# Four interleaved attention and linear-attention layers on one core: value products streamed twice, first products repeated, the last key tile alone, priorities moved

## The chip, the core and the metric

The kernel runs on one core of a Trainium2 chip. A core has TensorE (PE in the rows, its weight loads PEld), VectorE (DVE), ScalarE (ACT), GpSimd (POOL) and SyncE (SP, which here only issues DMAs). Each engine works through its own program in order and waits on semaphores for the others. TensorE's clock is granted at one of two levels, 2.4 GHz (1.00 in the rows) or 1.2 GHz (0.50). The metric is the device time of one execution in microseconds.

## What is computed

Activations are 2048 tokens by 512 features in bf16, 32 heads of 16. Two kinds of layer alternate twice, each with a layer norm ahead of it, an output projection and a residual sum behind it:

```python
def A(x):                      # 4 segments of 512 tokens
    q, k, v = x @ wq, x @ wk, x @ wv        # by head
    for s in range(4):
        p = softmax(q_s @ k_s.T * scale + causal mask)
        a_mem = (phi(q_s) @ M) / (phi(q_s) @ z + 1e-6)
        o_s = g * a_mem + (1 - g) * (p @ v_s)
        M, z = M + phi(k_s).T @ v_s, z + sum(phi(k_s))
    return o @ wo
def B(x):                      # all 2048 tokens at once
    q, k, v = split(x @ wqkv)
    f = lambda t: concat(softmax(t @ w_phi), softmax(-t @ w_phi))
    kv, z = f(k).T @ v, sum(f(k))           # over all tokens
    return (f(q) @ kv) / (f(q) @ z + 1e-6) @ wo
x = x + A(norm(x)); x = x + B(norm(x))
x = x + A(norm(x)); x = x + B(norm(x))
```

B needs `kv` and `z` of all 2048 tokens before its first query can be finished, so each pair of layers (L = 0 and L = 1 in the code) has one point where everything waits for the last key tile.

## The kernel before

A token tile is 128 tokens; there are 16, four to a segment. The program is not written in the order in which it runs. `build` records operations in a graph (`Graph.op`), each with engines it may run on, a duration in ns, the tiles that it reads and writes, and a label. `Graph.schedule` plays the graph through a planner: `backward` gives each operation a priority, `forward` lets each engine take the ready operation of best priority whose tiles can be had, and the best of 12 rounds for each of six rules fixes the order of every engine's program. So a changed duration, or a changed priority, moves instructions anywhere.

Products go through `mm`: a list of pairs, one product on the array's lower and one on its upper 64 rows, which run together. In `a_att` the scores of query tile `i` against key tile `j` (label S) are one pair of 512 columns, `D<-pQ,pK` in the rows; ScalarE makes the exponential of 1024 columns of it (`act`, L577), GpSimd masks the diagonal tile (L1005), and the value products (label PV, `D<-pV,p`) have the probabilities as weights and 16 value columns and a column of ones as the moving side: 17 columns for each head, key tile and half, 5120 products in all. VectorE then takes the reciprocal of the sums (L623) and scales (L1033). A PSUM tile `D` has two halves of 512 columns; of a half a PV product group uses the first 136 columns, and where there is a memory term 136 more.

`b_keys` makes the keys and values of B: projections `D<-WB_k,pX` and `D<-WB_v,pX` of two token tiles at a time, exponentials of both signs (label kexp), their sums by head (Zred, L1107), reciprocals (rZ, L623), the scaled values (Vt, L1118), and the products `D<-pT,p` that are summed into `KV32` (L1081). `TOK` says which pairs of tiles of a segment go together: in segments 0 to 2 all four tiles, in segment 3 the first pair, then the second. `b_query` makes the query exponentials (`D<-pX,WB_q`), the denominators (`D<-Rz,p`), the numerators (`D<-Rkv,p`) of each tile, scales them (L1194, L1201) and hands them to `out_proj`, whose products are `D<-WB_o,p` (for A `D<-WA_o,p`). The residual of B is added on VectorE (L1066) for even tiles; for the odd ones (`RES_PE`) TensorE adds it as a fifth product with the identity (`D<-X,ident`), and a copy by ScalarE or VectorE takes the sum back to `X`.

While it plays, `forward` keeps count of the columns that TensorE has streamed lately. Where they are few and the operation is a score pair, the pair is issued twice (`o.again`); the second issue computes the same again. In this program that happens to 24 pairs.

Of the kernel before, what the change touches and what calls it, by code (L numbers as in the profile page):

```python
# [9 lines left out]
ALU = mybir.AluOpType  # L10
# [82 lines left out]

WINDOW, KEEP = 3000.0, 0.45


class Graph:
# [39 lines left out]
    def op(self, ch, reads=(), writes=(), opens=(), kind="c", lat=None, label="", ndma=0, port=False, kb=0, hard=()):  # L137
        o = Op()
        o.id = len(self.ops)
        o.ch = ch  # L140
        o.deps = set()
        o.succ = []
        o.tiles = []
        o.opens = list(opens)
        o.kind = kind
        o.lat = lat
        o.label = label
        o.ndma = ndma
        o.need = False
        o.port = port  # L150
        o.kb = kb
        o.hard = tuple(hard)
        o.cyc = o.again = 0
        o.deps.update(hard)
# [73 lines left out]
    def forward(self, prio, pools, rule):  # L228
# [72 lines left out]
        while len(order) < n:  # L301
# [25 lines left out]
            for e in ENGS:  # L327
# [39 lines left out]
                if e == "pe":  # L367
                    while seen_pe and seen_pe[0][0] < now - WINDOW:
# [37 lines left out]
    def schedule(self, pools, rounds, off):  # L406
# [3 lines left out]
        for rule in RULES:  # L410
# [10 lines left out]
            self.log.append(min(log))  # L421
        self.model_us = self.forward(best[1], pools, best[2]) / 1000.0


    def emit(self):
# [108 lines left out]
class Kernel:  # L534
# [20 lines left out]
    def mm(self, phases, cols, reads, writes, opens=(), label="", after=None):  # L555
# [5 lines left out]
        for n, cs in enumerate(cols):  # L561
            dur = sum(max(c / 2.4 + 2.5, 25.5) for c in cs)

            def fn(e, n=n):
                ins = None
                for pair in phases()[n] * (1 + cell[n].again):
                    for out_ap, lhsT, rhs, st, sp in pair:
                        ins = e.matmul(out_ap, lhsT, rhs, start=st, stop=sp, tile_position=(basep(lhsT), 0))  # L568
                return ins
            last = self.g.op({"pe": (dur, fn)}, reads, writes, opens if n == 0 else (), label=label, hard=(last,) if last else ())  # L570
            last.cyc = sum(cs)
            cell.append(last)
        return last
# [51 lines left out]
    @staticmethod  # L625
    def dur_recip(n):
        return 65 + 6.3 * n

# [190 lines left out]
    def ln(self, t, xT, flex=False, pe=False, root="pool"):  # L819
        R, v = self.R, self.v  # L820
        tt = t % 4
        v(lambda e: e.bn_stats(self.stats[:, t, :], self.X[:, t, :]), 602, [R("X", t)], [R("st", t)], label="bn")  # L822
        v(lambda e: e.bn_aggr(self.mv[:, t, :], self.stats[:, t, :]), 75, [R("st", t)], [R("mv", t)], label="bn")  # L823
        rs = self.rstd[:, t:t + 1]
# [10 lines left out]
        if flex:  # L835
# [3 lines left out]
            self.g.op({"dve": (323, lambda e: e.tensor_scalar(xn.t[:], self.X[:, t, :], self.mv[:, t, 0:1], rs, op0=ALU.subtract, op1=ALU.mult)),  # L839
                       "act": (590, lambda e: e.activation(xn.t[:], self.X[:, t, :], ACT.Identity, scale=rs, bias=nb))},  # L840
                      [R("X", t), R("mv", t), R("rstd", t), R("nb", t)], [xn], label="xn", port=True)
# [23 lines left out]

    def vproj(self, ps, W, wres, tts, xT, opens=(), label=""):
        self.proj(ps, lambda b, h, k: (xT.t[64 * h:64 * h + 64, k, tts[b] * 128:tts[b] * 128 + 128], W[64 * h:64 * h + 64, k, :]), 512,
                  [xT[tt] for tt in tts] + wres, opens, label)
# [107 lines left out]
    def a_att(self, L, s, i):  # L976
# [9 lines left out]
        for hp in range(2):  # L986
# [22 lines left out]
            def phases(PV=PV, PTs=PTs, hp=hp, pvv=pvv):  # L1009
# [17 lines left out]
            self.mm(phases, [[17] * (8 * (i + 1)) + ([68, 4, 68, 4] if nm else []), [17] * (8 * (i + 1))],  # L1027
                    list(PTs.values()) + [PTs[(gg, i)][hh] for gg in range(2) for hh in range(2)] + [VT[j] for j in range(i + 1)]
# [62 lines left out]
    def b_keys(self, L, c, parts):  # L1091
# [4 lines left out]
        for part in parts:  # L1096
            Es, Vts = {}, {}
            for tp in part:
                tts = (2 * tp, 2 * tp + 1)
                S = self.T(self.pD, "gen")  # L1100
                E = Es[tp] = [self.T(self.p2, "ET") for _ in range(2)]
                Z = self.T(self.pS, "Z")
                self.vproj(S, self.WB["k"], [R("WB", "k", i) for i in range(4)], tts, xT, opens=E + [Z], label="BK")
                for sgn in range(2):
                    self.act(lambda sgn=sgn, E=E: E[sgn].t[:], lambda S=S: S.t[:], ACT.Exp, 1024, [S], [E[sgn]],
                             scale=1.0 - 2.0 * sgn, label="kexp")
                    fn = lambda e, sgn=sgn, E=E, Z=Z: e.tensor_reduce(Z.t[:, sgn * 64:(sgn + 1) * 64],  # L1107
                                                                      E[sgn].t[:].rearrange("p (h d) -> p h d", d=16), AX.X, ALU.add)
                    v(fn, 1131, [E[sgn]], [Z[sgn]], label="Zred")
                for b, tt in enumerate(tts):  # L1110
                    Vt = Vts[tt] = self.T(self.pT, "Vt")
                    v(lambda e, Vt=Vt, Z=Z, b=b: self.recip(e, Vt.t[:, :, :, 16, :], Z.t[:, 0:128].rearrange("p (s t g h) -> p s t g h", s=2, t=2, g=NG)[:, :, b]),
                      self.dur_recip(64), [Z[0], Z[1]], [Vt["z"]], label="rZ")
                ps = self.T(self.pD, "gen")
                self.vproj(ps, self.WB["v"], wv + [Vts[tt]["z"] for tt in tts], tts, xT, label="BV")
                for b, tt in enumerate(tts):
                    Vt = Vts[tt]
                    v(lambda e, Vt=Vt, ps=ps, b=b: e.tensor_tensor(  # L1118
                        Vt.t[:, :, :, 0:16, :],
                        ps.t[:, None, b * 512:b * 512 + 512].to_broadcast([128, 2, 512]).rearrange("p s (g d h) -> p s g d h", g=NG, h=8),  # L1120
                        Vt.t[:, :, :, 16:17, :].to_broadcast([128, 2, NG, 16, 8]), ALU.mult), 1131,
                      [ps, Vt["z"]], [Vt["v"]], label="Vt")
            tts = [2 * tp + b for tp in part for b in range(2)]
            for q in range(2):
# [3 lines left out]
                def phases(ps=ps, n=n, s0=s0, tts=tts, Es=Es, Vts=Vts):  # L1128
                    def item(b, h, k, tt, ph):
                        sl = s0 + b * n + k  # L1130
                        return (ps.t[:, 512 * b + k * 136:512 * b + k * 136 + 136],
                                Es[tt // 2][sl % 2].t[64 * h:64 * h + 64, (tt % 2) * 512 + (sl // 2) * 128:(tt % 2) * 512 + (sl // 2 + 1) * 128],
                                Vts[tt].t[64 * h:64 * h + 64, sl % 2, sl // 2, :, :].rearrange("p c h -> p (c h)"),
                                ph == 0 and k == 0 and tt == tts[0], ph == 1 and k == n - 1 and tt == tts[-1])
                    return [[(item(p, 0, k, tt, p), item(1 - p, 1, k, tt, p)) for k in range(n) for tt in tts] for p in range(2)]
                self.mm(phases, [[136] * (n * len(tts))] * 2, [E for tp in part for E in Es[tp]] + [Vts[tt][r] for tt in tts for r in "zv"], [ps], label="KV")
                self.kv_add(ps, q, c == 0 and part[0] == 0, c == 3 and part[-1] == 1)

# [118 lines left out]


def basep(ap):
    st = ap.ap[0][0]  # L1260
# [13 lines left out]
ROUNDS = 12  # L1274
OFF = {"warm": 1e6}
N_WARM = 14
# [38 lines left out]
```

## Time and profile before

| | us |
|---|---|
| median of three runs | 574.87 |
| lowest, highest | 570.24, 577.41 |
| the profiled execution | 577.28 |
| its span, first to last instruction | 575.5 |

The profiled execution stands at the upper end of the runs, 0.4% over their median. Its granted clock, taken over the span, is 0.938 of full speed. A busy share is an average over stages that differ: the start (loads and folding of weights) to some 100 us, attention of the first pair of layers to 240, the point where B waits for its last keys at 260, attention of the second pair to 510 with B's queries of the first in it, the second such point at 534, and B's queries and outputs to the end.

### The profile page before, as it was taken

What the parts mean: (1) busy time and instruction counts of PE and PEld (TensorE: products, weight loads), DVE (VectorE), ACT (ScalarE), POOL (GpSimd) and SP (SyncE); (2) the same over time, 40 slices, a digit from 0 to 9 for tenths busy, and PEclk for the clock granted to TensorE, in tenths of its full rate; (3) what the DMA queues carried; (4) which work ended last, traced back from release to release, by engine and by line L of the source; (5) the groups of instructions that cost most, each with busy time, mean ns of one, the idle gap of its engine ahead of it and who ended that gap; (6) DMA issues with size and microseconds to landing.
All of it is one profiled execution on the core that took longest, in us unless ns stands there. A gap on an engine that the chain in (4) does not pass through costs nothing.

```text
span 575.5 us, 24135 instructions
## 1 busy us (share of the span) xinstructions
PE 487.9 (85%) x10888; PEld 278.5 (48%) x10888; DVE 443.8 (77%) x858; ACT 462.2 (80%) x534; POOL 230.6 (40%) x401
## 2 busy tenths in 40 slices
PE   8788878889899888988798899887988997899776
PEld 3234344444455454446545455453544564345564
DVE  5979878996885957687898877796876885377794
ACT  4969878897999988757799798897987898856663
POOL 5757656426635643001255435651743373110000
PEclk9978889998999999997799898898998999699699
DMA  7294335334111111000124335322121013000245
GB/s 213 50 237 56 85 46 91 52 57 51 27 31 31 31 42 19 2 2 3 44 65 89 75 66 68 66 49 56 40 40 34 17 25 45 1 11 2 40 110 131
DMA packets 90517, 31.72 MB, mean 55 GB/s; under 512 B 77584, under 2 KB 90416, under 8 KB 90416
## 3 DMA queue, kind: packets, MB, share of 16 engines
q1 hardware_dynamic: 90352, 30.17, 26.8%
q8 instruction: 85, 1.39, 1.1%
q14 instruction: 16, 0.13, 0.1%
q0 software_dynamic: 64, 0.02, 0.0%
HBM read 6.32 MB, written 2.10 MB: 15 GB/s over the span
## 4 chain that ended last, share of the span: by engine, by line
PE 48%; DVE 20%; ACT 18%; DMA 9%; issue 4%; POOL 1%; SPq 0%; ACTq 0%; DVEq 0%
PE D L568 46%; ACT p L577 16%; DMA p<-p 7%; DMA pX<-p 2%; DVE p L586 2%; DVE X L1066 2%; DVE stats L822 2%; DVE p L1033 2%; PE D L887 2%; DVE pV L586 1%; DVE p L1194 1%; DVE pQ L939 1%; DVE p L843 1%; DVE pS L623 1%; DVE pS L1107 1%
## 5 line engine op out<-in xcount | busy, mean ns | idle before, releaser
L577 ACT ACTIVATE p<-D 128x1024 bf16<-128x1024 f32 x416 | 400.0, 1036 | 78.3 <-PE D L568 75.2
L1005 POOL TENSOR_SCALAR_AFFINE_SELECT p<-p 128x512 bf16<-128x512 bf16 x256 | 162.1, 659 | 165.9 <-ACT p L577 165.3
L568 PE MATMUL D<-pQ,pK 64*128 64x512 bf16 x688 | 131.3, 399 | 19.3 <-ACT p L577 14.2
L568 PE MATMUL D<-pV,p 64*128 64x17 bf16 x5312 | 92.7, 170 | 4.8 <-issue 3.3
L568 PEld LDWEIGHTS D<-pV,p 64*128 64x128 bf16 x5312 | 82.9, 93 | 18.3 <-issue 6.5
L568 PEld LDWEIGHTS D<-pQ,pK 64*128 64x128 bf16 x688 | 33.4, 96 | 58.8 <-ACT p L577 35.0
L830 POOL TENSOR_SCALAR rstd<-mv 128x1 f32<-128x1 f32 x60 | 17.6, 295 | 100.5 <-DVE mv L823 98.5
L1107 DVE TENSOR_REDUCE pS<-p 128x64 f32<-128x1024 bf16 x32 | 38.3, 1210 | 19.4 <-ACT p L577 19.3
L1066 DVE TENSOR_TENSOR X<-X,D 128x512 bf16<-128x512 bf16 x48 | 32.8, 683 | 26.5 <-PE D L568 26.0
L568 PE MATMUL D<-WA_o,p 64*128 64x256 bf16 x512 | 40.6, 278 | 12.6 <-DMA p<-p 6.8
L568 PE MATMUL D<-WB_o,p 64*128 64x256 bf16 x512 | 41.5, 288 | 9.6 <-DMA p<-p 7.6
L1033 DVE TENSOR_TENSOR p<-D,pS 128x256 bf16<-128x256 f32 x112 | 46.5, 419 | 2.5
L822 DVE BATCH_NORM_STATS2 stats<-X 128x6 f32<-128x512 bf16 x64 | 43.4, 683 | 5.8 <-DMA X<-in_A_x_dram 3.1
L1118 DVE TENSOR_TENSOR pT<-D,pT 128x1024 bf16<-128x1024 f32 x32 | 38.6, 1214 | 6.3 <-PE D L568 6.0
L568 PE MATMUL D<-WB_k,pX 64*128 64x512 bf16 x256 | 34.6, 389 | 6.8 <-issue 4.2
L568 PE MATMUL D<-WA_v,pX 64*128 64x512 bf16 x256 | 36.8, 412 | 3.6 <-DMA pX<-p 1.4
L623 DVE RECIPROCAL pS<-D 128x32 f32<-128x32 f32 (+1 forms) x64 | 20.8, 326 | 21.8 <-PE D L568 21.1
L832 POOL TENSOR_TENSOR rstd<-rstd,mhalf 128x1 f32<-128x1 f32 x60 | 35.6, 595 | 3.8
L568 PEld LDWEIGHTS D<-WA_o,p 64*128 64x128 bf16 x512 | 22.6, 96 | 29.3 <-DMA p<-p 11.3
L568 PE MATMUL D<-WB_v,pX 64*128 64x512 bf16 x256 | 32.8, 378 | 1.5 <-issue 0.7
L568 PE MATMUL D<-pX,WA_q 64*128 64x512 bf16 x224 | 32.6, 416 | 1.5 <-DVE p L1033 0.6
L568 PE MATMUL D<-pX,WB_q 64*128 64x512 bf16 x256 | 33.6, 392 | 0.2
(110 smaller groups left out, 647.6 us busy)
## 6 DMA issues: line engine op xcount, KB each, us to landing
pQ<-p SPq DMA_DIRECT2D x112, 32.0 KB, 1.8
out_dram<-X SPq DMA_DIRECT2D x16, 128.0 KB, 1.9
X<-in_A_x_dram SPq DMA_DIRECT2D x3, 512.0 KB, 6.0
pX<-in_B_wqkv_dram SPq DMA_DIRECT2D x3, 512.0 KB, 5.5
p<-p SPq DMA_TRANSPOSE x76, 2.8
pX<-p SPq DMA_TRANSPOSE x54, 2.7
X<-in_A_x_dram SPq DMA_DIRECT2D x4, 128.0 KB, 2.2
pX<-in_A_wk_dram SPq DMA_DIRECT2D x2, 256.0 KB, 3.7
```

Of the source, the lines that this page charges most:

```text
L568: ins = e.matmul(out_ap, lhsT, rhs, start=st, stop=sp, tile_position=(basep(lhsT), 0))
L577: return self.g.op({"act": (dur, lambda e: e.activation(out_ap(), in_ap(), func, scale=scale))}, reads, writes, opens, label=label)
L586: "dve": ((340 if fast else n / 0.96 + 65), lambda e: e.tensor_copy(out_ap(), in_ap()))}
L623: return e.reciprocal(o, i)
L822: v(lambda e: e.bn_stats(self.stats[:, t, :], self.X[:, t, :]), 602, [R("X", t)], [R("st", t)], label="bn")
L830: v(lambda e: e.tensor_scalar(rs, self.mv[:, t, 1:2], LN_EPS, None, op0=ALU.add), 170, [R("mv", t)], [R("rstd", t)], eng="pool", label="rstd")
L832: v(lambda e: e.tensor_tensor(rs, rs, self.mhalf[:], ALU.pow), 540, [R("rstd", t), R("mhalf")], [R("rstd", t)], eng="pool", label="rstd")
L1005: v(lambda e, pt4=pt4: e.affine_select(pt4(), pt4(), [[0, 4], [1, 128]], ALU.is_ge, 0.0, base=0, channel_multiplier=-1), 560, [PT], [PT[hh ...
L1033: v(lambda e, pvv=pvv, rden=rden, part=part, dst=dst, k=k: e.tensor_tensor(part(dst), pvv()[:, :, k, :, 0:16], rden()[:, :, k, :, None].to ...
L1066: self.v(lambda e: e.tensor_tensor(xt(), xt(), res(), ALU.add), 602, [R("X", t), ps], [R("X", t)], label="res")
L1107: fn = lambda e, sgn=sgn, E=E, Z=Z: e.tensor_reduce(Z.t[:, sgn * 64:(sgn + 1) * 64], E[sgn].t[:].rearrange("p (h d) -> p h d", d=16), AX.X ...
L1118: v(lambda e, Vt=Vt, ps=ps, b=b: e.tensor_tensor(Vt.t[:, :, :, 0:16, :], ps.t[:, None, b * 512:b * 512 + 512].to_broadcast([128, 2, 512]). ...
```

## The change

- A value product streams its 17 columns twice. `twice` gives the moving side a second pass (step 0) and the output a second place 272 columns further on, in columns of the same half that nothing else uses and nobody reads. The products stay 5120, of 34 columns each.
- The planner may repeat any operation whose first pair has 64 columns or more, not only scores: its first pair is issued up to `again` times ahead of the real products, which begin with a start flag and so overwrite it. At most 1024 columns are added to one operation; the planner's own mark (`KEEP`) rises from 0.45 to 0.6, and the value products count with 34 columns.
- In segment 3 `b_keys` works with tiles 12 and 13 as a pair and 14 alone, then 15 alone.
- `RES_PE` holds for all tiles of B, even ones too.
- A few durations of the planner are set anew, and the best priorities are moved by 108 recorded random steps (`STEPS`), so the order is another one throughout.

```diff
-WINDOW, KEEP = 3000.0, 0.45
+WINDOW, KEEP, MORE = 3000.0, 0.6, 2
...
-                    o.again = int(o.label == "S" and now > WINDOW and streamed < KEEP * WINDOW * 2.4)
-                    dur *= 1 + o.again
-                    cyc = o.cyc * (1 + o.again)
+                    o.again = 0
+                    if o.unit >= 64:
+                        lack = KEEP * WINDOW * 2.4 - streamed - o.cyc
+                        o.again = min(MORE * 512 // o.unit, max(0, int(-(-lack // o.unit))))
+                    dur += o.again * (o.unit / 2.4 + 2.5)
+                    cyc = o.cyc + o.again * o.unit
...
+        prio, rule = best[1], best[2]
+        for seed in STEPS:
+            prio = self.moved(prio, seed)
...
-                for pair in phases()[n] * (1 + cell[n].again):
+                pairs = phases()[n]
+                for pair in [tuple(m[:4] + (True,) for m in pairs[0])] * cell[n].again + pairs:
...
-                    return (PV.t[:, c:c + 17], half(PTs[(gg, j)].t, h)[:, (4 * b + hl) * 128:(4 * b + hl + 1) * 128],
-                            half(VT.t, h)[:, j, 16 * hp + 8 * gg + 4 * b + hl, :], ph == 0 and not nm and ends[0], ph == 1 and ends[1])
+                    return (twice(PV.t[:, c:c + 17], 272), half(PTs[(gg, j)].t, h)[:, (4 * b + hl) * 128:(4 * b + hl + 1) * 128],
+                            twice(half(VT.t, h)[:, j, 16 * hp + 8 * gg + 4 * b + hl, :], 0), ph == 0 and not nm and ends[0], ph == 1 and ends[1])
...
+def twice(x, step):
+
+    return bass.AP(tensor=x.tensor, offset=x.offset, ap=[x.ap[0], [step, 2]] + list(x.ap[1:]))
...
-TOK = {0: ((0, 1),), 1: ((0, 1),), 2: ((0, 1),), 3: ((0,), (1,))}
+PAIRS = (((0, 1), (2, 3)),)
+TOK = {0: PAIRS, 1: PAIRS, 2: PAIRS, 3: (((0, 1), (2,)), ((3,),))}
...
-RES_PE = {(L, t) for L in range(2) for t in range(1, 16, 2)}
+RES_PE = {(L, t) for L in range(2) for t in range(16)}
```

The first place is on TensorE, in the last segment of the second pair of layers, where in the trace the scores of the fourth query tile stand (484 to 497 us). Before:

```order
L568 MATMUL D<-WB_k,pX 128x512 x8
L568 MATMUL D<-pQ,pK 128x512 x2
L568 MATMUL D<-WB_k,pX 128x512 x8
L568 MATMUL D<-pQ,pK 128x512 x16
L568 MATMUL D<-MSb,p 128x68 x2
L568 MATMUL D<-eps,onesb 128x4 x2
...
L568 MATMUL D<-pV,p 128x17 x128
L568 MATMUL D<-pX,WB_q 128x512 x8
```

Now:

```order
L593 MATMUL D<-pQ,pK 128x512 x4
L593 MATMUL D<-WA_o,p 128x256 x8
L593 MATMUL D<-pQ,pK 128x512 x2
L593 MATMUL D<-WA_o,p 128x256 x8
L593 MATMUL D<-MSb,p 128x68 x2
...
L593 MATMUL D<-pV,p 128x2x17 x64
L593 MATMUL D<-pQ,pK 128x512 x4
L593 MATMUL D<-pV,p 128x2x17 x64
L593 MATMUL D<-WB_k,pX 128x512 x8
L593 MATMUL D<-pQ,pK 128x512 x2
```

Eight score pairs stood in a row with nothing between them; now projections stand between short runs of scores, and the value products are cut in two.

The second place is on TensorE too, at the end of the keys of the second pair of layers (520 to 535 us). `D<-pT,p` are the key-value products, `D<-Rz,p` the first products that need all of them. Before:

```order
L568 MATMUL D<-pT,p 128x136 x48
L568 MATMUL D<-pX,WB_q 128x512 x16
L568 MATMUL D<-WB_v,pX 128x512 x32
L568 MATMUL D<-pX,WB_q 128x512 x8
L568 MATMUL D<-pT,p 128x136 x24
L568 MATMUL D<-pX,WB_q 128x512 x16
L568 MATMUL D<-pT,p 128x136 x40
L568 MATMUL D<-Rz,p 128x2x4 x64
```

Now:

```order
L593 MATMUL D<-WB_k,pX 128x256 x16
L593 MATMUL D<-pX,WB_q 128x512 x16
L593 MATMUL D<-WB_v,pX 128x256 x16
L593 MATMUL D<-pX,WB_q 128x512 x8
L593 MATMUL D<-WB_v,pX 128x256 x16
L593 MATMUL D<-pT,p 128x136 x36
L593 MATMUL D<-pX,WB_q 128x512 x8
L593 MATMUL D<-pT,p 128x136 x24
L593 MATMUL D<-pX,WB_q 128x512 x8
L593 MATMUL D<-pT,p 128x136 x4
L593 MATMUL D<-pX,WB_q 128x512 x8
L593 MATMUL D<-Rz,p 128x2x4 x64
```

The last two tiles are projected singly, one behind the other, and some query projections have moved behind the first `D<-Rz,p`.

The third place is on TensorE behind the same point of the first pair of layers (259 to 270 us). Before:

```order
L568 MATMUL D<-Rz,p 128x2x4 x64
L568 MATMUL D<-Rkv,p 128x64 x48
L568 MATMUL D<-Rz,p 128x2x4 x64
L568 MATMUL D<-Rkv,p 128x64 x32
L568 MATMUL D<-ident,p 128x64 x32
L568 MATMUL D<-WB_o,p 128x256 x16
```

Now:

```order
L593 MATMUL D<-Rz,p 128x2x4 x64
L593 MATMUL D<-Rkv,p 128x64 x132
L593 MATMUL D<-Rz,p 128x2x4 x64
L593 MATMUL D<-Rkv,p 128x64 x44
L593 MATMUL D<-ident,p 128x64 x48
L593 MATMUL D<-Rkv,p 128x64 x16
```

The numerator products (16 to a tile) and the transposes with the identity have repeated pairs ahead of them.

## Rows read from the trace of the kernel before

**Rows 1.** The page: busy time by engine, and each engine's share of the chain.

```profile
PE 487.9 (85%) x10888; PEld 278.5 (48%) x10888; DVE 443.8 (77%) x858; ACT 462.2 (80%) x534; POOL 230.6 (40%) x401
PE 48%; DVE 20%; ACT 18%; DMA 9%; issue 4%; POOL 1%; SPq 0%; ACTq 0%; DVEq 0%
```

**Rows 2.** Busy time of each engine by stage; PEclk, DMA share and GB/s stand last.

```profile
100.00:240.00 140.00, 122.53 (x3018) 69.66 (x3014) 110.85 (x197) 123.14 (x132) 59.34 (x104) 0.99 0.21 36
...
285.00:510.00 225.00, 196.09 (x4454) 110.56 (x4450) 170.43 (x330) 194.00 (x208) 103.31 (x181) 0.94 0.26 48
...
535.00:575.50 40.50, 28.73 (x768) 22.10 (x768) 27.56 (x63) 22.80 (x38) 0.00 (x0) 0.87 0.44 100
```

**Rows 3.** The same of the stretches at half clock: first, three, last, sum.

```profile
30.64:34.05 3.41, 3.41 (x18) 1.38 (x19) 3.41 (x9) 2.30 (x3) 1.52 (x3) 0.50 1.04 338
...
262.74:269.57 6.83, 4.92 (x114) 3.59 (x108) 6.13 (x13) 4.51 (x9) 0.00 (x0) 0.50 0.01 2
276.40:283.22 6.82, 5.11 (x108) 3.13 (x102) 6.31 (x18) 4.17 (x9) 0.77 (x2) 0.50 0.36 81
...
535.81:546.05 10.24, 7.88 (x240) 5.98 (x234) 7.74 (x20) 7.29 (x14) 0.00 (x0) 0.50 0.18 43
sum 71.70, PE 63.91 PEld 32.47 DVE 53.59 ACT 46.92 POOL 18.78; mean PE 3.99 PEld 2.03 DVE 3.35 ACT 2.93 POOL 1.17
```

**Rows 4.** Who waited for whom: total us, times, longest.

```profile
ACT p L577 <- PE D L568: 75.2, 72, 4.5
...
DVE X L1066 <- PE D L568: 26.0, 21, 2.7
```

**Rows 5.** TensorE's groups just ahead of falls at 436.82, 494.85 and 535.81.

```profile
L568 PE MATMUL D<-pV,p 64*128 64x17 bf16 x138 | 2.1, 167 | 0.0
...
L568 PE MATMUL D<-pQ,pK 64*128 64x512 bf16 x10 | 1.8, 392 | 2.1 <-ACT p L577 2.1
...
L568 PE MATMUL D<-Rz,p 64*128 64x8 bf16 x64 | 1.0, 163 | 1.3 <-DVE Rz L1087 1.3
```

**Rows 6.** The timeline of TensorE, bursts of short products: start, us, what.

```profile
258.99 0.95 PE L568 MATMUL D<-Rz,p 64*128 64x8 bf16 x64 [1.54 <-DVE Rz L1087]
...
260.19 0.89 PE L568 MATMUL D<-Rkv,p 64*128 64x64 bf16 x48 [0.25 <-DVE Rkv L1084]
...
264.23 0.61 PE L568 MATMUL D<-ident,p 64*128 64x64 bf16 x16 [0.81 <-ACT pS L577]
...
433.60 0.75 PE L568 MATMUL D<-pV,p 64*128 64x17 bf16 x48
...
436.84 0.89 PE L568 MATMUL D<-pV,p 64*128 64x17 bf16 x54 [0.98 <-issue]
```

**Rows 7.** Groups by line and form: busy us, mean ns, idle before and releaser.

```profile
L577 ACT ACTIVATE p<-D 128x1024 bf16<-128x1024 f32 x416 | 400.0, 1036 | 78.3 <-PE D L568 75.2
...
L1107 DVE TENSOR_REDUCE pS<-p 128x64 f32<-128x1024 bf16 x32 | 38.3, 1210 | 19.4 <-ACT p L577 19.3
...
L568 PE MATMUL D<-pX,WB_q 64*128 64x512 bf16 x256 | 33.6, 392 | 0.2
...
L1066 DVE TENSOR_TENSOR X<-X,D 128x512 bf16<-128x512 bf16 x48 | 32.8, 683 | 26.5 <-PE D L568 26.0
...
L623 DVE RECIPROCAL pT<-pS 128x64 bf16<-128x64 f32 x32 | 16.1, 528 | 1.9 <-PE D L568 1.8
...
L585 ACT ACTIVATE X<-D 128x512 bf16<-128x512 f32 x8 | 4.8, 596 | 6.8 <-PE D L568 6.8
```

**Rows 8.** The timeline at the end of the keys, 523 to 529 us.

```profile
523.23 4.10 PE L568 MATMUL D<-WB_v,pX 64*128 64x512 bf16 x32
...
525.41 4.87 DVE L1118 TENSOR_TENSOR pT<-D,pT 128x1024 bf16<-128x1024 f32 x4 [0.97 <-PE D L568]
...
528.24 2.08 ACT L577 ACTIVATE p<-D 128x1024 bf16<-128x1024 f32 x2 [3.58 <-PE D L568]
```

More of the change, by code (lines that the diff above doesn't have):

```diff
@@ L367, in forward @@
                 if e == "pe":
-                    while seen_pe and seen_pe[0][0] < now - WINDOW:
+                    while seen_pe and seen_pe[0][0] < now + dur - WINDOW:
                         streamed -= seen_pe.pop(0)[1]
-                    o.again = int(o.label == "S" and now > WINDOW and streamed < KEEP * WINDOW * 2.4)
-                    dur *= 1 + o.again
-                    cyc = o.cyc * (1 + o.again)
+                    o.again = 0
[4 more added lines that the diff above has]
+                    cyc = o.cyc + o.again * o.unit
                     seen_pe.append((now + dur, cyc))
@@ L421, in schedule, with moved @@
             self.log.append(min(log))
-        self.model_us = self.forward(best[1], pools, best[2]) / 1000.0
+        prio, rule = best[1], best[2]
+        for seed in STEPS:
+            prio = self.moved(prio, seed)
+        self.rule, self.prio = rule, prio
+        self.model_us = self.forward(prio, pools, rule) / 1000.0
+    def moved(self, prio, seed):
+        if not hasattr(self, "names"):
+            self.names = sorted({o.label for o in self.ops})
+            self.name = np.array([self.names.index(o.label) for o in self.ops])
+        r = np.random.RandomState(seed)
+        p = np.array(prio)
+        kind, label = r.randint(3), r.randint(len(self.names))
+        at, width, size = p[r.randint(len(p))], np.exp(r.uniform(6.5, 10.6)), np.exp(r.uniform(5.0, 8.7))
+        pick = np.abs(p - at) < width
+        if kind == 0:
+            pick &= self.name == label
+        elif kind == 1:
+            pick &= r.rand(len(p)) < 0.1
+        p[pick] += r.normal(0.0, size, pick.sum() if kind == 2 else 1)
+        return p
     def emit(self):
@@ L571, in mm @@
             last.cyc = sum(cs)
+            last.unit = cs[0] if n == 0 else 0
             cell.append(last)
@@ L1026, in phases @@
                 return [first + r[0], r[1]]
-            self.mm(phases, [[17] * (8 * (i + 1)) + ([68, 4, 68, 4] if nm else []), [17] * (8 * (i + 1))],
+            self.mm(phases, [[34] * (8 * (i + 1)) + ([68, 4, 68, 4] if nm else []), [34] * (8 * (i + 1))],
                     list(PTs.values()) + [PTs[(gg, i)][hh] for gg in range(2) for hh in range(2)] + [VT[j] for j in range(i + 1)]
@@ L1115, in b_keys @@
                 self.vproj(ps, self.WB["v"], wv + [Vts[tt]["z"] for tt in tts], tts, xT, label="BV")
-                for b, tt in enumerate(tts):
+                for tt in tts:
                     Vt = Vts[tt]
[L1118 to L1123, printed above, removed]
+                    if two:
+                        src = lambda ps=ps, c=512 * (tt - tts[0]): ps.t[:, None, c:c + 512].to_broadcast([128, 2, 512]).rearrange(
+                            "p s (b g d h) -> p s b g d h", b=2, g=2, h=8)
+                    else:
+                        src = lambda ps=ps: ps.t[:].rearrange("p (b c) -> p b c", b=2)[:, None, :, 0:256].to_broadcast([128, 2, 2, 256]).rearrange(
+                            "p s b (g d h) -> p s b g d h", g=2, h=8)
+                    vt = lambda Vt, c0, c1: Vt.t[:, :, :, c0:c1, :].rearrange("p s (b g) d h -> p s b g d h", b=2)
+                    v(lambda e, Vt=Vt, src=src, vt=vt: e.tensor_tensor(vt(Vt, 0, 16), src(), vt(Vt, 16, 17).to_broadcast([128, 2, 2, 2, 16, 8]), ALU.mult),
+                      1131, [ps, Vt["z"]], [Vt["v"]], label="Vt")
+            tts = [tt for ts in part for tt in ts]
+            last = part is parts[-1]
             for q in range(2):
@@ L1135, in phases @@
                     return [[(item(p, 0, k, tt, p), item(1 - p, 1, k, tt, p)) for k in range(n) for tt in tts] for p in range(2)]
-                self.mm(phases, [[136] * (n * len(tts))] * 2, [E for tp in part for E in Es[tp]] + [Vts[tt][r] for tt in tts for r in "zv"], [ps], label="KV")
-                self.kv_add(ps, q, c == 0 and part[0] == 0, c == 3 and part[-1] == 1)
+                self.mm(phases, [[136] * (n * len(tts))] * 2, list({E: 0 for tt in tts for E in Es[tt][0]}) + [(Vts[tt], ALLKEYS) for tt in tts], [ps], label="KV")
+                self.kv_add(ps, q, c == 0 and part is parts[0], c == 3 and last)
     def b_query(self, L, c, store):
```

38 lines of the change are left out of this document (26 added, 12 removed), and 10 rows, old and new, of the table STEPS.

## The prediction

> **What bounds the kernel now.** I read the page first. No engine is full: TensorE 85%, ScalarE 80%, VectorE 77% of the span, and the chain that ended last runs through all three, 48% TensorE, 20% VectorE, 18% ScalarE [rows 1]. So nothing is bounded by one engine's work, and a second off one engine is worth a part of a second. By stages the two attention stretches are ScalarE's: it is busy 123.14 of 140 us in the first and 194.00 of 225 us in the second [rows 2], mostly with 1036 ns exponentials [rows 7]. What it waits for is almost always TensorE: 75.2 us in 72 waits, the longest 4.5 us [rows 4]. The last 40.5 us, queries and outputs of B, have no full engine: TensorE 28.73, VectorE 27.56, ScalarE 22.80 [rows 2].
>
> Then I looked at the clock. TensorE runs at 1.2 GHz in 16 stretches of together 71.70 us [rows 3]. The three longest lie right behind the two points at which everything waits for the last keys. What TensorE did just before a fall is of three kinds [rows 5]: bursts of value products of 17 columns (138 of them), scores paced by ScalarE (five pairs with 2.1 us of waiting), and the short `D<-Rz,p` products after the keys. Few columns were streamed in all three. In the first kind the engine was not idle; it had narrow work.
>
> **What the slow clock costs.** In the slow stretches TensorE is busy 63.91 of 71.70 us; at full clock that work would take 32 us less at most. That is the upper bound, and much of it would come out as waiting. A better measure is ScalarE, the engine that attention waits for: it is busy 46.92 us there, 65%, and (462.2 - 46.92) / (575.5 - 71.7) = 82% elsewhere [rows 1, 3]. At 82% the same work takes 57 us, so the slow clock costs about 14.8 us. How much goes? The first kind of stretch is what the doubled value products aim at. The two points behind the keys get repeats in the first pair of layers (by the order, the third place: 84 repeated pairs of numerators) and few in the second. The waits between scores get repeats only where the planner foresaw the wait, and a place where the chip is late against the plan gets none. I take half: -7.4 us, between 0 and -14.8.
>
> **What the value products cost.** At full clock 24 pairs of 17 columns take 0.75 us; less the last product's own 0.17 us that is 25 ns from pair to pair. 32 pairs of 8 columns take (0.95 - 0.16) / 31 = 25 ns, also with an output in two runs of four columns, and 24 pairs of 64 columns (0.89 - 0.17) / 23 = 31 ns [rows 5, 6]. So a pair costs 25 ns from 8 to 17 columns, and at 64 columns 6 ns more. 34 columns lie between: 0 to 6 ns for 2560 pairs, 0 to 15 us of TensorE. I take 0, since 8 and 17 columns cost the same: width does not yet tell there. At half clock 17 columns take (0.89 - 0.17) / 26 = 28 ns and 64 take up to (0.61 - 0.17) / 7 = 63 ns [rows 6], so there the doubling may cost some ns, in the few stretches that stay slow.
>
> One rule speaks against this. The Trainium skill (PSUM — Partial Sum Buffer, Specifications) says that any non-contiguous access pattern slows matmuls significantly, for cache lines of 8 bytes; the new output is two runs of 17 columns, 272 apart. The 25 ns of `D<-Rz,p`, with its two runs, is against it here. By the rule the sum would come out on the other side; the third rival below has the price.
>
> **What the other added products cost.** By the order 185 pairs are now repeated, 146 of 64 columns, 15 of 256 and 24 of 512, where 24 of 512 were. A pair of 64 costs 31 ns; 16 pairs of 512 take 4.10 us with their gaps [rows 8], 0.25 us each, so one of 256 about 0.12. The new ones cost 146 x 0.031 + 15 x 0.12 = 6.3 us of TensorE. They stand where the planner saw room, so I count a quarter, 1.6 us. The residual of even tiles adds 32 pairs of 256 columns, 3.8 us, of which the chain's share of 48% counts [rows 1]: 1.8 us. Together about +3 us, between 0 and +10.
>
> **The last key tile.** In the end stretch the chain from the last keys' projection is: exponential 1.04, two sums of 1.21, two reciprocals of 0.53 and scaled values (four stand in a row, 4.87 us, while ScalarE waits 3.58 us) [rows 7, 8]. With a pair the part behind the first exponential's start is 1.04 + 2.42 + 1.06 + 2.43 = 6.9 us. With one tile it is an exponential of 512 columns, about 0.60 as for a copy of 512 [rows 7], two sums of half length, 1.21, one reciprocal, 0.53, one set of values, 1.22: 3.6 us. The gain is 3.3 us at each of two points if VectorE is the chain there. In the second pair of layers tiles 14 and 15 are projected one behind the other (second place), so two sets of values stand together again: 2 us there. I take -5, between 0 and -6.6. At 0 it would be because TensorE has query projections to do there anyway; they then fill the time that the shorter chain frees, or move behind the point, as some have.
>
> **The residual.** 16 additions of 683 ns leave VectorE (10.9 us) and 16 copies come, 6 to VectorE and 10 to ScalarE at 596 ns [rows 7]. VectorE's additions waited 26.0 us for TensorE, more than they took [rows 4], so they are where waits end, not what makes them. -1 us, between +2 and -3.4 (half of VectorE's net 6.8).
>
> **The new order.** No row prices it. What it can take back is ScalarE's idle time in the attention stretches: 16.9 + 31.0 = 47.9 us [rows 2], less the 7.4 that the clock has been given, so 40 us at most. It works where projections stand between scores, as at the first place, because the long run of scores there left TensorE idle behind ScalarE and then ScalarE idle behind 128 value products. But the order is fixed by a plan, and each engine goes through it without regard to what is late. A bad turn costs a wait of the kind that is there now, 4.5 us at the longest [rows 4]; two net would be +9. I take a quarter of 40: -10, between +9 and -25.
>
> **The sum.** -7.4 + 0 + 3 - 5 - 1 - 10 = -20.4 on the profiled 577.28: 556.9. That execution stands 0.4% over the median, so against 574.87 I say 555.
>
> **The rivals.**
> First, the order gains nothing on the chip: the planner's gain lies in places where its durations and the chip's differ, and TensorE's waits move instead of going. Then -7.4 + 3 - 5 - 1 is -10, and -7 with half the clock's gain lost: 565 to 568. For it: 75.2 us of waits come in 72 pieces, so no single place gives much. Against it: they are 75.2 of the 78.3 us that the exponentials stood idle [rows 7], one kind of wait between the same two engines, which an order can act on.
> Second, the order and the clock both come off: with -14.8 for the clock and -20 for the order the sum is -38, 537 after the 0.4%. For it: 48 us of idle ScalarE in two stages that no dependence forces. Against it: two points behind the keys remain, with transposes by DMA, 9% of the chain [rows 1], that nothing here shortens.
> Third, slower: a value product with two output runs costs two products. 50 ns for 25 is +64 us of TensorE in 2560 pairs; at its 48% of the chain +31 us, and the sum is +10: 585. It lies in all attention, the bursts of 128 becoming 3.2 us long, with ScalarE waiting behind each. It decides from 20.4 / (2560 x 0.48) = 17 ns more a pair: there the rest of the gain is gone. The page's rule named above would act this way; for it there is the longer jump between the runs, against it the `D<-Rz,p` row.
> Fourth, the clock stays as it is, because the chip's delays put the gaps elsewhere than planned: 0 for the clock gives 563; this is inside the forecast's own range.
>
> **How the numbers follow.** Forecast, 545 to 565 with the likeliest at 555: 0.53. First rival (565 to 578): 0.20. Second (533 to 545): 0.18. Third, and an order that loses more than all else gains: 0.09. About 2% is what a measurement of this kernel can tell from no change; faster by that is under 563.4: the second rival and most of the forecast, 0.69. Slower is over 586.4: 0.05. Within 2%: 0.26. The range takes in the forecast, most of the first rival and over half of the second: 539 to 574.
>
> **What the profile of the changed kernel would show.** Clock: mean granted clock from 0.938 to 0.96 or 0.97, with fewer slow stretches in attention and a shorter one at 260 us. Value products: 24 pairs in 0.75 us still; if the same bursts take over 0.9 us the third rival is at work. Keys: one `Vt` less between the last projection and `D<-Rz,p`, and ScalarE's 3.58 us wait there shorter. Order: ScalarE's wait for TensorE down from 75.2 to about 60 us, its share in the second attention stretch from 86% to 90%. The forecast fails if that wait is unchanged with the clock up (then the clock was not what ScalarE waited for), or if new waits of VectorE or of the DMA transposes take its place.

## The result, and the profile after

The changed kernel takes 548.93 us (median of four runs, 540.75 to 550.73) against 574.58 us: ratio 0.9488, 95% interval 0.933 to 0.9646. That ratio leaves out two of the four runs, the profiled one among them, as disturbed; the same kernel measured again in six runs gives 548.45 us against 577.09 us on that chip, ratio 0.9561 (0.9493 to 0.963), and the experiments below stand beside that one. It is faster by 4.4 to 5.1%; 555 us were forecast.

The page of the changed kernel, busy time by engine and shares of the chain, as in [rows 1]:

```profile
PE 477.3 (87%) x11338; PEld 287.7 (53%) x11338; DVE 438.2 (80%) x853; ACT 470.6 (86%) x547; POOL 231.5 (42%) x401
PE 47%; DVE 21%; ACT 20%; DMA 6%; issue 4%; SPq 1%; POOL 0%; DVEq 0%; ACTq 0%
```

The work is nearly what it was and the chain has the same make-up. The span is shorter because the engines stand idle less: ScalarE's share went from 80% to 86% with 8 us more work. Who waited for whom, as in [rows 4]:

```profile
ACT p L603 <- PE D L593: 48.1, 54, 4.5
...
DVE X L1096 <- PE D L593: 14.6, 11, 3.8
```

ScalarE's wait for TensorE fell by 27 us, about as much as the span. The stretches at half clock, first, the longest and the sum of seven, as in [rows 3]:

```profile
34.78:38.20 3.42, 3.42 (x18) 1.30 (x20) 2.87 (x8) 1.02 (x1) 0.00 (x0) 0.50 1.02 351
...
509.24:516.07 6.83, 5.93 (x182) 5.12 (x176) 4.40 (x10) 4.87 (x9) 0.00 (x0) 0.50 0.18 41
...
sum 24.37, PE 22.95 PEld 15.02 DVE 12.39 ACT 11.90 POOL 1.97; mean PE 3.28 PEld 2.15 DVE 1.77 ACT 1.70 POOL 0.28
```

71.70 us have become 24.37. That looks like the cause; the experiments say that it is the smaller part. TensorE's timeline at the first place of the change, the fourth query tile of the last segment, answers to [rows 6]:

```profile
472.83 0.98 PE L593 MATMUL D<-pV,p 64*128 64x34 bf16 x64
473.64 0.61 PE L593 MATMUL D<-pQ,pK 64*128 64x512 bf16 x4
474.07 0.98 PE L593 MATMUL D<-pV,p 64*128 64x34 bf16 x64
```

32 pairs of 34 columns take 0.98 us, (0.98 - 0.17) / 31 = 26 ns from pair to pair, where 17 columns took 25: the second pass is all but free. Two score pairs now stand between the bursts, and ScalarE's exponentials of them start at 474.07 us, with the second burst.

It helps most to cut the span at four events of TensorE: the start of the last product of attention's output projection (`D<-WA_o,p`) and the first product of the denominators (`D<-Rz,p`), once for each pair of layers. Busy time by stage of the changed kernel:

```profile
0.00:229.18 229.18, 197.05 (x4522) 111.13 (x4523) 194.72 (x372) 201.70 (x226) 122.82 (x207) 0.99 0.32 70
229.18:245.25 16.07, 15.10 (x216) 8.35 (x210) 11.55 (x19) 10.78 (x12) 0.77 (x2) 1.00 0.01 2
245.25:488.21 242.96, 215.70 (x5428) 133.18 (x5430) 194.59 (x388) 216.59 (x248) 107.12 (x190) 0.98 0.25 47
488.21:503.94 15.73, 14.98 (x214) 7.92 (x209) 12.71 (x21) 10.20 (x13) 0.79 (x2) 1.00 0.01 2
503.94:547.26 43.32, 34.50 (x974) 27.16 (x972) 24.63 (x56) 31.37 (x51) 0.00 (x0) 0.92 0.39 94
```

The same cuts of all profiled runs, in us, with the time at half clock. "Keys" is the stretch between the two events.

| run | attention 1 | keys 1 | queries 1, attention 2 | keys 2 | last stage | span | half clock |
|---|---|---|---|---|---|---|---|
| before | 234.6 | 24.4 | 252.0 | 22.9 | 41.6 | 575.5 | 71.7 |
| changed | 229.2 | 16.1 | 243.0 | 15.7 | 43.3 | 547.3 | 24.4 |
| changed, again | 231.8 | 16.1 | 240.8 | 15.7 | 44.1 | 548.5 | 27.3 |
| once | 237.0 | 16.1 | 237.8 | 15.7 | 43.2 | 549.8 | 27.3 |
| neither | 238.3 | 16.1 | 235.2 | 15.7 | 40.9 | 546.2 | 51.2 |
| no_repeat | 233.7 | 16.1 | 235.4 | 15.7 | 41.9 | 542.9 | 27.7 |
| before_twice | 230.1 | 24.4 | 249.1 | 22.9 | 40.5 | 567.0 | 58.4 |
| no_steps | 235.7 | 20.4 | 243.3 | 18.8 | 44.5 | 562.6 | 17.1 |
| no_steps_pair | 234.6 | 20.7 | 240.5 | 20.9 | 41.4 | 558.1 | 13.7 |
| no_steps_odd | 234.5 | 21.3 | 238.5 | 17.4 | 43.1 | 554.9 | 20.5 |
| no_steps_pair_odd | 233.2 | 23.3 | 249.4 | 21.2 | 42.9 | 569.9 | 30.7 |
| quarter_steps | 236.2 | 16.2 | 244.9 | 17.2 | 43.9 | 558.3 | 24.0 |
| half_steps | 232.4 | 16.0 | 240.2 | 17.5 | 43.5 | 549.6 | 20.4 |
| repeat_not_b | 231.1 | 16.1 | 239.7 | 15.7 | 45.1 | 547.7 | 24.4 |

Of the 28.2 us of span, 15.5 came from the two stretches of the keys, 14.4 from attention; the last stage gave 1.7 back.

### The profile page after: what moved, and what is told of

It is laid out like the page before. It is cut to its first block, busy times and chain, and to the rows that moved or that the text cites. A ratio compares the mean times of both kernels' runs of the same rounds, so it can differ in the third digit from the quotient of the medians.

```text
span 547.3 us, 25035 instructions
## 1 busy us (share of the span) xinstructions
PE 477.3 (87%) x11338; PEld 287.7 (53%) x11338; DVE 438.2 (80%) x853; ACT 470.6 (86%) x547; POOL 231.5 (42%) x401
## 4 chain that ended last, share of the span: by engine, by line
PE 47%; DVE 21%; ACT 20%; DMA 6%; issue 4%; SPq 1%; POOL 0%; DVEq 0%; ACTq 0%
PE D L593 47%; ACT p L603 18%; DMA p<-p 4%; DVE p L612 2%; DVE stats L848 2%; DVE p L1063 2%; DVE p L869 2%; DVE pQ L969 1%; DVE pS L1141 1%; DVE X L1096 1%; SPq L975 1%; DVE pK L612 1%; DVE pS L649 1%; DMA pX<-p 1%; DVE p L1236 1%
## 5 line engine op out<-in xcount | busy, mean ns | idle before, releaser
L603 ACT ACTIVATE p<-D 128x1024 bf16<-128x1024 f32 (+1 forms) x420 | 400.6, 1026 | 52.1 <-PE D L593 48.1
L593 PE MATMUL D<-pQ,pK 64*128 64x512 bf16 x676 | 125.0, 381 | 15.5 <-ACT p L603 11.0
L593 PE MATMUL D<-pV,p 64*128 64x34 bf16 x5312 | 94.3, 177 | 5.5 <-issue 2.8
L1141 DVE TENSOR_REDUCE pS<-p 128x64 f32<-128x1024 bf16 (+1 forms) x36 | 38.7, 1087 | 6.6 <-ACT p L603 6.6
L593 PE MATMUL D<-WB_k,pX 64*128 64x512 bf16 (+1 forms) x288 | 34.6, 353 | 4.6 <-issue 2.7
L593 PE MATMUL D<-pX,WA_q 64*128 64x512 bf16 x228 | 30.8, 390 | 5.1 <-DMA pX<-p 2.2
L593 PE MATMUL D<-WB_v,pX 64*128 64x512 bf16 (+1 forms) x290 | 34.0, 354 | 0.8 <-DVE pT L649 0.4
L593 PEld LDWEIGHTS D<-WA_o,p 64*128 64x128 bf16 x532 | 23.9, 94 | 19.0 <-DMA p<-p 5.5
L1096 DVE TENSOR_TENSOR X<-X,D 128x512 bf16<-128x512 bf16 x32 | 21.8, 681 | 15.0 <-PE D L593 14.6
L593 PE MATMUL D<-pX,WB_q 64*128 64x512 bf16 x256 | 32.1, 376 | 0.1
```

Source lines behind the costliest of these rows:

```text
L603: return self.g.op({"act": (dur, lambda e: e.activation(out_ap(), in_ap(), func, scale=scale))}, reads, writes, opens, label=label)
L1096: self.v(lambda e: e.tensor_tensor(xt(), xt(), res(), ALU.add), 602, [R("X", t), ps], [R("X", t)], label="res")
L1141: fn = lambda e, sgn=sgn, ev=ev, Z=Z, nz=nz: e.tensor_reduce(Z.t[:, sgn * nz:(sgn + 1) * nz], ev().rearrange("p (h d) -> p h d", d=16), AX ...
```

## The experiments

Theory after the result: the added columns hold TensorE's clock up, and the clock is a good part of the gain. Rival: the order makes the gain, and the clock rises along with it. All runs after the first are edits of the changed kernel unless said otherwise. They come from three chips: `after_again`, `once`, `neither` and `before_twice` from one, the runs without steps from a second, and `no_repeat`, `repeat_not_b`, `quarter_steps` and `half_steps` from a third. The median of the kernel before is 577.1, 577.1 and 577.8 us on them, with single executions from 568 to 583.

**The changed kernel again.** No edit.

> The changed kernel as it is, on the chip of the next three, so that they have a like to stand beside. Both theories: 0.95 of the kernel before, within 1%, and a granted clock of 0.975 to 0.99.

548.45 us, ratio 0.9561 (0.9493 to 0.963), clock 0.975: as expected.

**once, neither, no_repeat.** The order of every engine is kept to the instruction; only what TensorE streams within an operation is changed.

```diff
 # once, neither
-                    return (twice(PV.t[:, c:c + 17], 272), half(...),
-                            twice(half(VT.t, h)[...], 0), ...)
+                    return (PV.t[:, c:c + 17], half(...),
+                            half(VT.t, h)[...], ...)
 # neither, no_repeat
-                for pair in [tuple(m[:4] + (True,) for m in pairs[0])] * cell[n].again + pairs:
+                for pair in pairs:
```

> The changed kernel's order on every engine, but a value product streams its 17 columns once; the repeats stay. If the doubled columns hold the clock up (theory): falls behind bursts of value products come back, granted clock 0.955 to 0.97, 3 to 8 us over the changed kernel. If the order makes the gain and the clock rises with it (rival): granted clock and time within 0.01 and 2 us of the changed kernel. If the second run of 17 columns costs TensorE time: up to 5 us under it.

> The changed kernel's order, value products streamed once and no product repeated: 185 pairs fewer. If the clock is held up by the added columns: granted clock 0.94 to 0.955, 7 to 15 us over the changed kernel (my term was 7.4, with 14.8 for all slow stretches). If it is the order: clock above 0.97 and the time the same or 1 to 3 us less, since 6 us of TensorE's work are gone.

> The changed kernel's order with value products streamed twice, but no product repeated. In the run with neither, slow clock cost the first attention stretch 6.5 us and missing repeats gave back 3 to 5 us behind it. If the two are separate (theory): first stretch 230 to 233 us as with both, last stretch 40.5 to 41.5 us as with neither, 3 to 6 us under the changed kernel and the fastest so far. If the repeats are what holds the clock in the first stretch (rival): it is 236 us or more and the total is that of the changed kernel.

Once: 551.99 us, 0.9615 (0.9535 to 0.9694). Neither: 548.58 us, 0.9578 (0.9513 to 0.9643). No_repeat: 544.59 us, 0.9453 (0.9405 to 0.9502). The four cells of columns and repeats:

| | 17 columns | 34 columns |
|---|---|---|
| no repeats | 548.6 | 544.6 |
| repeats | 552.0 | 548.5 |

The doubled columns take away 3.5 to 4.0 us in either row, the repeats add 3.4 to 3.9 us in either column, and together they come to nothing. No_repeat is from another chip than the other three cells; by the ratios it is 7 us, not 4.0, under neither. The intervals of neither and no_repeat do not overlap; those of the other pairs do, so what stands behind the repeats' cost is that it came twice, not one clear difference. My theory that the added columns carry the gain falls: without any of them the kernel is as fast as with all. Yet the clock was held up by them in the profiled executions. The slow stretches of neither, first, last and sum of ten:

```profile
28.73:38.97 10.24, 6.97 (x34) 2.42 (x34) 9.06 (x20) 4.38 (x6) 4.00 (x6) 0.50 0.59 187
...
510.01:516.84 6.83, 6.23 (x164) 4.91 (x166) 5.03 (x12) 5.90 (x10) 0.00 (x0) 0.50 0.24 61
sum 51.19, PE 44.47 PEld 23.73 DVE 38.95 ACT 34.34 POOL 14.09; mean PE 4.45 PEld 2.37 DVE 3.90 ACT 3.43 POOL 1.41
```

51.19 us against 24 to 28 in the three others, so either addition alone holds it about as well as both. The profiled execution of once has the 27.3 us of the changed kernel, measured again, and is still 1.2 us slower (3.5 us by the medians); so in that row the gain of the columns is not tied to less slow clock in all. One fall of once, at 230.09 us, does stand right behind 128 value products, as the theory expected. ScalarE is busy 34.34 of the 51.19 us of neither, 67%, as the 65% of [rows 3]. Three stages of no_repeat show where that pays, beside the same three of neither. No_repeat:

```profile
0.00:233.74 233.74, 197.17 (x4472) 110.31 (x4474) 195.57 (x372) 201.75 (x226) 122.68 (x207) 0.97 0.30 69
...
249.80:485.23 235.43, 209.08 (x5192) 127.63 (x5194) 195.01 (x388) 215.52 (x248) 107.77 (x190) 0.98 0.26 49
...
500.97:542.94 41.97, 32.11 (x890) 24.73 (x888) 24.61 (x56) 31.34 (x51) 0.00 (x0) 0.95 0.48 96
```

Neither:

```profile
0.00:238.30 238.30, 203.49 (x4471) 112.49 (x4472) 195.84 (x372) 202.07 (x226) 123.01 (x207) 0.94 0.29 68
...
254.37:489.54 235.17, 209.74 (x5192) 128.57 (x5194) 195.09 (x388) 215.63 (x248) 108.06 (x190) 0.97 0.25 49
...
505.27:546.18 40.91, 33.00 (x890) 25.63 (x888) 24.58 (x56) 31.51 (x51) 0.00 (x0) 0.92 0.45 99
```

The granted clock of the first stage is 0.97 for 0.94, TensorE is busy 6.3 us less with as many products, and the stage is 4.6 us shorter. The two later stages are 0.3 and 1.1 us longer. In the other row the first stage gains too: 237.0 us in once, 231.8 in the changed kernel again. No_repeat's first and last stage are 0.7 and 0.5 us over what was expected; its total is as expected.

**before_twice.** The kernel before, in its own order, with `twice` in the value products alone.

```diff
-                    return (PV.t[:, c:c + 17], half(...),
+                    return (twice(PV.t[:, c:c + 17], 272), half(...),
-                            half(VT.t, h)[...], ...)
+                            twice(half(VT.t, h)[...], 0), ...)
```

> The kernel before with its own order, only its value products stream twice into the spare columns. If added columns pay by themselves: the falls at 136, 399 and 437 us, which stood behind bursts of value products, go; granted clock 0.95 to 0.96, 3 to 7 us under the kernel before. If ScalarE did not wait for the clock: the clock rises and the time stays within 2 us.

568.79 us, 0.9941 (0.9902 to 0.9981): by the ratio 3.4 us, clock 0.948 for 0.938. At the low end of what was expected, and the same as in the new order. The falls at 139.9 us (called 136 above), 399 and 437 us are gone; twelve stretches of half clock remained, among them the three behind the keys. A new fall, at 300.36 us, stands behind 64 doubled value products and five score pairs, with TensorE busy for 2.63 us from 296.95 us on; so the doubled columns do not prevent every fall.

**repeat_not_b.** The numerators and transposes of B are not repeated; attention's repeats stay.

```diff
-                for pair in [...] * cell[n].again + pairs:
+                for pair in [...] * (0 if label in ("N", "otpp", "otp") else cell[n].again) + pairs:
```

> The changed kernel, but the numerators and the transposes of the pair sums in B are not repeated: 168 products of numerators and 80 of transposes fewer, none of them in attention. If those repeats cost time behind the keys, by their own length and by the wait for instructions there: last stretch 41 to 42 us against 43 to 44, 2 to 3 us under the changed kernel. If they hold the clock up there: last stretch 44 us or more, with more slow clock in it.

551.54 us, 0.9568 (0.952 to 0.9617), last stage 45.1 us. A miss in the total and in the last stage. The other reading, 44 us or more with more slow clock there, came in length only: 7.4 us of half clock for the changed kernel's 7.3. This stage streams all but the same products as no_repeat's (894 and 890 in the traces) and is 3.1 us longer, so one profile of it tells little of a difference of 2 us.

Right behind the keys, though, the timelines show a cost of these repeats. From the first denominators to the first output projection of the first pair of layers, in the changed kernel:

```profile
245.25 0.95 PE L593 MATMUL D<-Rz,p 64*128 64x8 bf16 x64 [0.83 <-DVE Rz L1117]
...
252.51 0.70 PE L593 MATMUL D<-ident,p 64*128 64x64 bf16 x36 [0.83 <-issue]
...
256.52 0.53 PE L593 MATMUL D<-Rz,p 64*128 64x8 bf16 x28 [1.71 <-issue]
...
257.51 1.69 PE L593 MATMUL D<-WB_o,p 64*128 64x256 bf16 x14
```

In no_repeat:

```profile
249.80 0.95 PE L593 MATMUL D<-Rz,p 64*128 64x8 bf16 x64 [0.83 <-DVE Rz L1117]
...
258.84 1.04 PE L593 MATMUL D<-WB_o,p 64*128 64x256 bf16 x8
```

In repeat_not_b:

```profile
247.14 0.95 PE L593 MATMUL D<-Rz,p 64*128 64x8 bf16 x64 [0.83 <-DVE Rz L1117]
...
256.17 1.69 PE L593 MATMUL D<-WB_o,p 64*128 64x256 bf16 x14
```

That is 12.3, 9.0 and 9.0 us; the changed kernel again has 11.7, once 12.1 and neither 9.0. Behind the second point it is 7.6 to 8.2 us in the three runs with B's repeats and 6.6 in the three without. So B's repeats delay the output projections by 2.7 to 3.2 us at the first point and by 1.1 to 1.6 at the second. How much of that reaches the end is not shown. In repeat_not_b 34 repeated pairs are left in the stage with the second attention, which takes 239.7 us for no_repeat's 235.4; what these cost by themselves was not tried.

**no_steps and its three variants.** The list of steps is empty. The variants put the keys of segment 3 back to pairs, the residual of even tiles back to VectorE, or both.

```diff
-STEPS = (20000105, ...)
+STEPS = ()
 # pair
-TOK = {..., 3: (((0, 1), (2,)), ((3,),))}
+TOK = {..., 3: (((0, 1),), ((2, 3),))}
 # odd
-RES_PE = {(L, t) for L in range(2) for t in range(16)}
+RES_PE = {(L, t) for L in range(2) for t in range(1, 16, 2)}
```

> The changed kernel with an empty list of steps, so that the planner's own best priorities stand; doubled columns, repeats, single last tile and all residuals on TensorE stay. If the moved priorities make the gain (theory, after the runs without added columns kept it): 0.975 to 1.0 of the kernel before, 12 to 25 us over the changed kernel. If the single last tile and the residual make it (rival): 0.955 to 0.97, with 15 to 17 us from the last output projection of attention to the first product of the denominators, as in the changed kernel, against 23 and 24 before.

> As the run without steps, and in segment 3 the keys go by pairs as before. If the single last tile shortens the way to the end of the keys: 5 to 8 us more than with it, in the two stretches from the last output projection of attention to the first denominator product. If the way is set by the order: those stretches are as long with and without.

> As the run without steps, and only odd tiles of B have the residual on TensorE. My term for the residual was 1 us, between 3.4 us of gain and 2 us of loss: time within 3 us of the run without steps. If VectorE was the bound of the last stage: 4 to 6 us more, all behind the second end of the keys.

> As the run without steps, with keys by pairs and the residual of odd tiles alone: what is left of the change are the added columns, the repeats and a few durations of the plan. If all rests on the moved priorities: the same as the run without steps, within 3 us. If keys and residual carry a part: 5 to 9 us over it, near the kernel before less the 3 us that doubled columns gave it.

No_steps 565.26 us, 0.9855 (0.9803 to 0.9907); pair 561.9, 0.9808 (0.9747 to 0.9868); odd 558.08, 0.972 (0.967 to 0.977); both 574.26, 0.9975 (0.9934 to 1.0016). Without the steps 16.8 us of the gain are gone, as the theory of the moved priorities expected; the two stretches that its rival put at 15 to 17 us are 20.4 and 18.8. Of the variants, odd misses: it is 7.2 us faster than no_steps and was to be within 3. In pair the two stretches are 2.4 us longer, neither the 5 to 8 us nor the none that were expected. Both is 9.0 us over no_steps, as expected if keys and residual carry a part; it still has the added columns, the repeats and the new durations, and is as slow as the kernel before. ScalarE waited for TensorE in no_steps:

```profile
ACT p L603 <- PE D L593: 59.3, 58, 4.5
```

The variants do not add up: the residual on TensorE is 7 us slower with a single last tile and 12 us faster with pairs. Each of these edits makes the planner lay out the whole program anew, and the four layouts lie up to 16 us apart. So the residual's worth cannot be read from them. What can be read is one stretch: the two stretches of the keys together are 39.2 us with the single tile and 41.6 with pairs, 38.8 and 44.5 with odd residuals. The single last tile is worth 2.4 to 5.7 us there; in the total it is 3.4 us slower with all residuals on TensorE and 16.2 faster with the odd ones. Less slow clock does not by itself make these runs fast: pair has the least of all, 13.7 us, and is 13.5 us slower than the changed kernel; both has 30.7 us where the kernel before has 71.7, and takes as long.

**quarter_steps, half_steps.** The first 27 or 54 of the 108 steps.

```diff
-        for seed in STEPS:
+        for seed in STEPS[:54]:
```

> The changed kernel with the first 54 of the 108 steps. The steps gave 17 us from none to all. If what the plan gains comes out on the chip by degrees: 553 to 559 us. If only few steps count, or the chip's gain is chance as from one plan to another (the three runs without steps differ by 16 us among themselves): anywhere from 548 to 568.

> The same with the first 27 steps. By degrees: 557 to 563 us, over the run with half. By chance: no order among none, quarter, half and all.

559.55 us, 0.9703 (0.9657 to 0.9748), with a quarter; 552.64 us, 0.9597 (0.9549 to 0.9645), with half. None, quarter, half, all: 565.3, 559.6, 552.6, 548.5. The four stand in the order that gain by degrees would give, quarter inside its range and half 0.4 us under it. The intervals of half and all overlap, and four values can fall into order by chance, so this speaks for a gain by degrees and does not settle it.

**What the order does at the keys.** TensorE's groups between the last `D<-WA_o,p` and the first `D<-Rz,p` of the first pair of layers. Before:

```profile
L568 PE MATMUL D<-pX,WB_q 64*128 64x512 bf16 x88 | 10.9, 377 | 0.1
L568 PE MATMUL D<-WB_v,pX 64*128 64x512 bf16 x48 | 6.0, 377 | 0.2
L568 PE MATMUL D<-pT,p 64*128 64x136 bf16 x128 | 5.4, 220 | 0.2
L568 PE MATMUL D<-WB_k,pX 64*128 64x512 bf16 x16 | 2.1, 376 | 0.0
```

Changed:

```profile
L593 PE MATMUL D<-pX,WB_q 64*128 64x512 bf16 x72 | 8.9, 376 | 0.0
L593 PE MATMUL D<-pT,p 64*128 64x136 bf16 x64 | 2.5, 220 | 0.0
L593 PE MATMUL D<-WB_v,pX 64*128 64x256 bf16 x32 | 2.4, 270 | 0.1
L593 PE MATMUL D<-WB_v,pX 64*128 64x512 bf16 x16 | 2.1, 377 | 0.0
L593 PE MATMUL D<-WB_k,pX 64*128 64x256 bf16 x16 | 1.2, 270 | 0.1
```

The stretch is mostly TensorE's in both kernels, with hardly any idle time ahead of a group (22.23 of 24.43 us busy before, 15.10 of 16.07 in the changed one); of the chain that ended last, TensorE has 75% in it before and 89% after. It is shorter because less stands in it: 24.4 us of these kinds before, summed with their overlaps, 17.1 after. Half the key-value products, and key and value projections of the earlier tiles, are now done in attention, where TensorE is idle for 32 of 229 us. It is the steps that moved the key-value products: in no_steps, with the single last tile, all 128 are in the stretch.

```profile
L593 PE MATMUL D<-pT,p 64*128 64x136 bf16 x128 | 4.8, 220 | 0.1
```

## Why the prediction was right, and which steps were off

The forecast of 555 us, its sign and its range held; -20.4 us were summed and -25.6 measured. That the sum came so near is in part luck: the order gave 6.8 us more than was summed for it, the added columns with the repeats gave nothing, and the residual is unknown. Step by step:

- **What bounds the kernel** held. No engine was full, the two attention stretches waited on TensorE handing scores to ScalarE, and the gain stands in that wait: 75.2 to 48.1 us, further than the 60 that I named. ScalarE's share of the stage with the second attention went from 85% (213.82 of 252.00 us) to 89%.
- **The clock** (-7.4): the mechanism is borne out in part, and the share was mis-sized. Half clock fell from 71.7 to 24.4 us, more than the half that I gave it. But the new plan without any addition brings it to 51.2; the added columns take the next 24 us. The price that I drew from ScalarE's busy share, 14.8 / 71.7 = 0.21 us for each slow microsecond, fits one pair of runs: 23.5 us less slow clock for 4.0 us between neither and no_repeat, 0.17. It is no constant: between once and the changed kernel again the first stage has 10.2 us less of it and is 5.2 us shorter, while the totals of slow clock in these two profiles are equal. The columns were worth 3.5 to 4 us; that all of it came by the clock is not shown.
- **The value products** (0) held: 26 ns a pair for 25. The third rival, in which two output runs cost two products, did not come. The Trainium skill (PSUM — Partial Sum Buffer, Specifications) says that any non-contiguous access pattern slows matmuls significantly. For two runs of 17 columns, 272 apart, that does not show (26 ns for 25), and the measurement decides.
- **The other added products** (+3, of which +1.6 for repeats): the repeats cost 3.4 to 3.9 us, but that is all 185 pairs, with the 24 of 512 columns that I had left out because the kernel before had as many. TensorE is busy 11.0 us more with them (479.4 us in the changed kernel again, 468.4 in no_repeat), so they cost about a third of that, and the quarter that I took was near. The 161 new pairs were not measured by themselves.
- **The last key tile** (-5): the size held for the single tile, 2.4 to 5.7 us, and the mechanism did not. I priced VectorE's sums and values behind the last projection; the chain through the stretch is mostly TensorE's products. How the single tile shortens it was not tried by itself. The stretches lost 15.5 us in all, since the order moves other products out of them as well.
- **The residual** (-1) is not settled: its sign changes with the plan. The last stage gained nothing, 43.3 us for 41.6, with 3.1 us of query projections moved into it (24 products of 512 columns, 12 pairs).
- **The new order** (-10): under-sized. It is worth 16.8 us. I had no row for it and took a quarter of ScalarE's idle time in attention; what I left out is that an order can also empty the stretches of the keys, where the steps take 7.4 of those 16.8 us (39.2 to 31.8). The 8 to 12 us that no_steps keeps over the kernel before (by the ratio and by the medians) are not taken apart by these runs.
- **Readings that were off.** A stretch of half clock among scores, at 494.85 us, is as long (6.83 us) as two of the three that I put behind the keys as the longest. Of the 84 repeated pairs of numerators 60 stand behind the first point and 24 behind the second, by the counts of the changed kernel and no_repeat. VectorE's additions waited 26.0 us for TensorE, less than the 32.8 that they took [rows 7]. The fourth rival's sum is 562, not 563.

The fastest version is no_repeat, 544.59 us, 0.9453 of the kernel before: the new order with doubled value products and no repeats. Its interval (0.9405 to 0.9502) just touches that of the changed kernel's second measurement (0.9493 to 0.963).

## What to carry to other kernels

When a change raises the clock and lowers the time, undo the clock's part with the order frozen before believing that one made the other: here the added columns gave some 4 us, and the repeated products took them back. Where a stretch waits for one last tile, look at how many products stand in it beside that tile's chain; moving the ones that could be done earlier gave more than shortening the chain. And where a planner lays out the program, an edit of the work is also a new layout (four of them lay up to 16 us apart here), so price an edit in a frozen order or in one stretch, not by totals.

## What the runs showed of the hardware that was not expected

TensorE's clock fell also while the engine was busy most of the time with products of few columns (from 433.41 us to the fall at 436.82 us it was busy 2.36 us, with 138 value products [rows 5]):

```profile
433.41:436.82 3.41, 2.36 (x158) 2.14 (x154) 3.10 (x5) 1.83 (x3) 1.16 (x3) 1.00 0.02 5
```

With a second pass over the same columns, at 26 ns a pair for 25, that fall and two like it went in before_twice. And TensorE waits inside a burst for nothing that the profile shows: in the second profile of the changed kernel, among the numerators of one tile (16 products, and 16 repeated ones ahead of them),

```profile
509.93 0.46 PE L593 MATMUL D<-Rkv,p 64*128 64x64 bf16 x19
512.18 0.53 PE L593 MATMUL D<-Rkv,p 64*128 64x64 bf16 x13 [1.80 <-issue]
```

1.80 us. In the 36 us behind the first keys the three runs with B's repeats have 2.5 to 3.1 us of such waits, neither and no_repeat none and repeat_not_b 0.3. What TensorE waited for was not tried.
